# A fused attention and SwiGLU kernel: exponents of double-precision weights on ScalarE, and one batch's sum of squares on TensorE

## The chip, the cores and the metric

The kernel runs on one core of a Trainium2 chip. The metric is the device time of one execution in microseconds (us). The engines are TensorE (PE, with its weight loads as PEld), VectorE (DVE), ScalarE (ACT), GpSimd (POOL) and SyncE (SP), which issues most DMAs.

## The reference

Eight batches of 512 tokens and 32 state rows attend to each other over 8 heads of 64; the 544 rows of each batch then go through an RMS norm and a SwiGLU layer of width 1536. Inputs x and state are float32. The weights reach the kernel as 64-bit floating point, so each weight is two 32-bit words.

```python
scores = scale * x @ state.T;  a = softmax(scores);   xread = a @ state
scores2 = scale * state @ x.T; a2 = softmax(scores2); sread = a2 @ x
x = concat([xread, sread], axis=2)        # (8, 8, 544, 64) -> (4352, 512)
xn = x / sqrt(mean(x * x, -1) + 1e-6) * rms_g
g = xn @ w_gate; val = xn @ w_val         # (512, 1536) each
out = (g * sigmoid(g) * val) @ w_out      # (1536, 512)
```

## The kernel before

**Weights.** The three weight matrices are cut into 18 pieces of 128 partitions by 1024 values: 12 for the gate and value matrices, 6 for the output matrix. `load_piece` brings a piece in as pairs of 32-bit words (tile `raw`, four buffers; the word with index 1 holds sign, 11 exponent bits and 20 mantissa bits, the word with index 0 the low mantissa). `to_float32` makes float32 of it: VectorE shifts the exponent out (L183), ScalarE turns it into the inverted float32 exponent by two Relus (L185, L186), and ScalarE copies the low word as a scaled float32 (L188). VectorE then extracts the top mantissa bits and sets the hidden one (L189), adds the low part (L190), puts the sign into the exponent (L192) and multiplies mantissa by power of two (L196). `top` and `ex` have two buffers each. The first piece is done in two halves. Gate and value pieces go to `w_m` tiles in SBUF (three buffers) and, by a DMA, to a float32 copy in DRAM (`w_d`), from which later batches load them; output pieces stay in `wo`. `ready(n)` converts pieces up to number n, and is called by the code that needs them.

**Attention.** `attention(b)` is a generator whose steps are placed between the matmuls of the batch before. It transposes x (L232), makes scores (L240), softmaxes both ways, reads the states (L291, into four PSUM banks: two named `at`, two named `pv`), squares the reads on ScalarE (L297) and sums the squares. VectorE adds the four squares (L300, L301), and TensorE multiplies by a column of ones (L304) to sum over partitions. VectorE adds the epsilon (L307), GpSimd takes the power (L206), TensorE spreads it (L209), and VectorE scales the attention weights by it (L310). The other direction follows (L316 to L346).

**Feed-forward.** `make_v` multiplies the states by the weights (L381) into the `pv` banks, and ScalarE copies the result to `v` (L388). In batch 0, `hidden` multiplies `v` with the scaled attention weights (L407), applies tanh on ScalarE (L412) and gates on VectorE (L413, L415); `project_as_ready` multiplies with `wo` (L493). Later batches use a form with seven products (L445, L536). So all conversions, and the attention of batches 0 and 1, fall into batch 0's stage, up to about 140 us of the trace.

**Order.** Tiles and waits are placed by the framework, which also orders each engine's instructions when the program is built. The order in the trace is therefore not the order of the text: in the trace L316 at 31.87 us runs ahead of L300 at 35.53 us. Each engine then works in order.

Of the kernel before, what the change touches and what calls it, by code (L numbers as in the profile page):

```python
# [8 lines left out]
F32 = mybir.dt.float32  # L9
I32 = mybir.dt.int32  # L10
U32 = mybir.dt.uint32
ALU = mybir.AluOpType
ACTF = mybir.ActivationFunctionType
AXX = mybir.AxisListType.X
# [2 lines left out]
P = 128  # L17
# [5 lines left out]
def kernel(  # L23
# [20 lines left out]
    VE, SE, GE, TE = nc.vector, nc.scalar, nc.gpsimd, nc.tensor  # L44
# [15 lines left out]
    two = ctx.enter_context(tc.tile_pool(name="two", bufs=2))  # L60
# [35 lines left out]
    ones = consts.tile([P, 1], F32, name="ones")  # L96
    GE.memset(ones, 1.0)
    bounds = consts.tile([P, 2], F32, name="bounds")
    GE.memset(bounds[:, 0:1], 1151.0)
    GE.memset(bounds[:, 1:2], 255.0 * (1 << 23))  # L100
    rms_g = consts.tile([P, NI], F32, name="rms_g")

# [26 lines left out]
    def home(k):  # L129
        if k >= NM:  # L130
            m = 2 * (k - NM)
            return wo[:, m:m + 2].rearrange("p m (i f) -> p m i f", f=P)
        mp = k // 2
        return (w_sb[mp] if k % 2 else new_w(mp))[:, :, :, k % 2, :]

    def load_piece(k):
        if k >= len(pieces):
            return
        src = pieces[k]
        if src.dtype == F32:  # L140
            return
        raw[k] = raws.tile([P, 8 * P, 2], I32, name="raw")
        out_ = raw[k].rearrange("p (a f) two -> p a (f two)", a=src.shape[1])
        for a in parts(k):
            nc.sync.dma_start(out=out_[:, a], in_=src[:, a].bitcast(I32))

    def parts(k):

        n = pieces[k].shape[1]
        return (slice(0, n // 2), slice(n // 2, n)) if k == 0 else (slice(0, n),)  # L150
# [3 lines left out]
    def ready(n):  # L154

        nonlocal n_ready
        while n_ready < min(n, len(pieces)):
            k = n_ready
            to_float32(k)
            if k < NM and k % 2:  # L160
                nc.sync.dma_start(out=w_d[k // 2], in_=w_sb[k // 2])
            n_ready += 1

    def to_float32(k):


        load_piece(k + RAW_AHEAD)
        to = home(k)
        if k not in raw:
            src = pieces[k].rearrange("p a (c f) -> p a c f", f=P)  # L170
            for a in range(src.shape[1]):
                nc.sync.dma_start(out=to[:, a], in_=src[:, a])
            return
        whole = raw.pop(k)
        tops = conv.tile([P, 8 * P], I32, name="top")
        exs = conv.tile([P, 8 * P], I32, name="ex")
        n = pieces[k].shape[1]
        for a in parts(k):
            cols = slice(8 * P * a.start // n, 8 * P * a.stop // n)
            r, top, ex, dst = whole[:, cols, :], tops[:, cols], exs[:, cols], to[:, a]  # L180
            hi = r[:, :, 1]
            man = r.bitcast(F32)[:, :, 0]
            VE.tensor_scalar(ex, hi, 20, 0x7ff, op0=ALU.logical_shift_right, op1=ALU.bitwise_and)  # L183

            SE.activation(out=ex, in_=ex, func=ACTF.Relu, scale=-1.0, bias=bounds[:, 0:1])  # L185
            SE.activation(out=ex, in_=ex, func=ACTF.Relu, scale=-float(1 << 23),  # L186
                          bias=bounds[:, 1:2])
            SE.activation(out=man, in_=r.bitcast(U32)[:, :, 0], func=ACTF.Copy, scale=2.0 ** -52)  # L188
            VE.tensor_scalar(top, hi, 0xfffff, 0x100000, op0=ALU.bitwise_and, op1=ALU.bitwise_or)  # L189
            VE.scalar_tensor_tensor(out=man, in0=top, scalar=2.0 ** -20, in1=man,  # L190
                                    op0=ALU.mult, op1=ALU.add)
            VE.scalar_tensor_tensor(out=ex, in0=hi, scalar=-(1 << 31), in1=ex,  # L192
                                    op0=ALU.bitwise_and, op1=ALU.bitwise_or)
            man, ex = (t.rearrange("p (a c f) -> p a c f", f=P, c=dst.shape[2])
                       for t in (man, ex.bitcast(F32)))
            VE.tensor_tensor(out=dst, in0=man, in1=ex, op=ALU.mult)  # L196


    stT_g = {}
# [3 lines left out]
    def inverse_rms(ss, n):  # L203

        ri = two.tile([P, NC], F32, name="ri")
        GE.tensor_tensor(out=ri[:, 0:n], in0=ss, in1=mhalf[:, 0:n], op=ALU.pow)  # L206
        rp = aps.tile([P, NC, P], F32, name="at")
# [4 lines left out]
    def attention(b):  # L212
        xb, packed = x_sb.pop(b), rows.pop(b)
        if b + 1 < B:
# [7 lines left out]
                     in_=packed.rearrange("p e d -> p (e d)"), identity=ident)  # L222
        VE.tensor_copy(stT, tp)
        VE.tensor_tensor(out=stT_g[b], in0=stT, in1=rms_g.unsqueeze(2).to_broadcast([P, 4, Ns]),
                         op=ALU.mult)
# [11 lines left out]
        sp = [aps.tile([P, S], F32, name="at") for e in range(2)]  # L237
        for j in range(4):
            for e in range(2):
                TE.matmul(out=sp[e][Ns * j:Ns * j + Ns, :], lhsT=stT[D * e:D * e + D, j, :],  # L240
                          rhs=xT[j // 2][D * e:D * e + D, j % 2].rearrange("p c t -> p (c t)"),
                          start=True, stop=True)
# [12 lines left out]
        for cp in range(2):  # L255
            tp = aps.tile([P, 2, 2, P], F32, name="at")
            for c in range(2):
                for e in range(2):
# [6 lines left out]
                             op=ALU.subtract)  # L265
# [4 lines left out]
        for cp in range(2):  # L270
# [6 lines left out]
                             op=ALU.mult)  # L277
            tp = aps.tile([P, 2, 2, P], F32, name="at")
            for c in range(2):
                for e in range(2):  # L280
                    TE.transpose(out=tp[:, c, e, :],
                                 in_=eS[:, 2 * cp + c, e].rearrange("p j n -> p (j n)"),
# [6 lines left out]
        for j in range(4):  # L289
            for e in range(2):  # L290
                TE.matmul(out=reads[j][D * e:D * e + D, :],  # L291
                          lhsT=packed[Ns * j:Ns * j + Ns, e, :],
                          rhs=aT[Ns * j:Ns * j + Ns, e].rearrange("n c t -> n (c t)"),
                          start=True, stop=True)
        sq = [one.tile([P, 2, S], F32, name="sq%d" % i, tag=("xT1", "eS")[i]) for i in range(2)]
        for j in (2, 3, 0, 1):
            SE.activation(out=sq[j // 2][:, j % 2, :], in_=reads[j], func=ACTF.Square,  # L297
                          scale=DM ** -0.5)
        yield
        VE.tensor_tensor(out=sq[1], in0=sq[1], in1=sq[0], op=ALU.add)  # L300
        VE.tensor_tensor(out=sq[0][:, 0, :], in0=sq[1][:, 0, :], in1=sq[1][:, 1, :], op=ALU.add)  # L301
        sp = aps.tile([P, NC], F32, name="at")
        for c in range(NC):
            TE.matmul(out=sp[:, c:c + 1], lhsT=sq[0][:, 0, P * c:P * c + P], rhs=ones,  # L304
                      start=True, stop=True)
        ss = two.tile([P, NC], F32, name="ss")
        VE.tensor_scalar(ss, sp, 1e-6, None, op0=ALU.add)  # L307
        yield
# [2 lines left out]
                         in1=rp.unsqueeze(1).to_broadcast([P, 2, S]), op=ALU.mult)  # L311
# [7 lines left out]
        for e in range(2):  # L319
            SE.activation(out=e2[:, e], in_=sS[:, e], func=ACTF.Exp, scale=SCALE,  # L320
                          bias=s2[:, e:e + 1], accum_out=z2[:, e:e + 1])
# [11 lines left out]
        for e in range(2):  # L333
            for c in range(NC):
                for j in range(4):
                    h = 2 * j + e
                    TE.matmul(out=rp[Ns * j:Ns * j + Ns, e, :],
                              lhsT=e2T[:, e, c, Ns * j:Ns * j + Ns],
                              rhs=xb[:, c, D * h:D * h + D],
                              start=(c == 0), stop=(c == NC - 1))  # L340
        sr = two.tile([P, 2 * D], F32, name="sr")
        for e in range(2):
            VE.tensor_scalar(sr[:, D * e:D * e + D], rp[:, e, :], z2[:, e:e + 1], None,
                             op0=ALU.mult)
# [266 lines left out]
    for k in range(1, RAW_AHEAD):  # L611
        load_piece(k)
    steps = attention(0)
    while next(steps) != "tokens":
        pass
    make_v(0, 0)
    ready(4)
    states_read = steps
    steps = attention(1)
    for _ in states_read:  # L620
        pass
# [5 lines left out]
    for b in range(B):  # L627
        if b > 0:
            steps = attention(b + 1) if b + 1 < B else state_norm()
        else:  # L630
            for m in range(NM):
                if m % 2 == 0 and m + 2 < NM:
                    make_v(b, m // 2 + 1)
                v, _ = v_sb[b, m // 2]
                hidden(m, S, lambda e, k: v[:, e, m % 2, k, :],
                       [aT_s[b][:, e, :] for e in range(2)])
                some(3)

            def between(m):
                if m == NM - 4:  # L640
                    ready(len(pieces))
                    early.close()
                    open_late()
                    prepare(b + 1)

            project_as_ready(store_tokens(b), between)
            sums = weight_sums()
# [53 lines left out]
```

## Time and profile before

| what | value |
|---|---|
| median of 4 runs | 879.05 us (877.03 to 881.34) |
| the profiled execution | 880.2 us, span 878.4 us |
| mean granted TensorE clock | 0.966 |
| TensorE busy | 832.3 us, 95% of the span |
| VectorE busy | 473.5 us, 54% |
| ScalarE busy | 341.7 us, 39% |

The profile is one execution taken by the hardware profiler. A group line gives the line of the kernel, the engine, the operation, out<-in with shapes, and how often it ran; then the busy time, the mean length of one in ns, and the engine's idle time before it with what ended it. The granted clock is the share of TensorE's full speed. A float32 matmul appears as two passes, each with a weight load.

### The profile page before, as it was taken

What the parts mean: (1) busy time and instruction counts of PE and PEld (TensorE: products, weight loads), DVE (VectorE), ACT (ScalarE), POOL (GpSimd) and SP (SyncE); (2) the same over time, 40 slices, a digit from 0 to 9 for tenths busy, and PEclk for the clock granted to TensorE, in tenths of its full rate; (3) what the DMA queues carried; (4) which work ended last, traced back from release to release, by engine and by line L of the source; (5) the groups of instructions that cost most, each with busy time, mean ns of one, the idle gap of its engine ahead of it and who ended that gap; (6) DMA issues with size and microseconds to landing.
All of it is one profiled execution on the core that took longest, in us unless ns stands there. A gap on an engine that the chain in (4) does not pass through costs nothing.

```text
span 878.4 us, 12043 instructions
## 1 busy us (share of the span) xinstructions
PE 832.3 (95%) x4806; PEld 610.0 (69%) x4806; DVE 473.5 (54%) x749; ACT 341.7 (39%) x571; POOL 156.2 (18%) x215
## 2 busy tenths in 40 slices
PE   3597999999999999999999999999999999999997
PEld 2252544577877778777877787777877787788886
DVE  5899898269216841476226921694148623651231
ACT  5678472364125520563136412552056313520110
POOL 0000005131113211230123112221132022310000
PEclk9598899999999999999999999999999999999999
DMA  9777771231233203330243124220243012311310
GB/s 291 251 203 256 216 280 49 99 140 52 50 112 129 96 18 118 112 141 4 73 130 134 52 49 144 99 93 1 85 141 112 1 56 97 141 44 37 108 48 25
DMA packets 61592, 94.11 MB, mean 107 GB/s; under 512 B 38752, under 2 KB 46432, under 8 KB 54624
## 3 DMA queue, kind: packets, MB, share of 16 engines
q1 hardware_dynamic: 57376, 92.29, 31.6%
q10 hardware_dynamic: 4160, 1.05, 0.5%
q8 instruction: 38, 0.62, 0.3%
q14 instruction: 18, 0.15, 0.0%
HBM read 78.12 MB, written 15.20 MB: 106 GB/s over the span
## 4 chain that ended last, share of the span: by engine, by line
PE 79%; DVE 11%; ACT 6%; DMA 1%; issue 1%; SPq 0%; POOL 0%; ACTq 0%; DVEq 0%
PE f L536 30%; PE f L445 24%; PE f L407 8%; PE pv L381 5%; PE f L493 5%; PE at L232 2%; ACT sq L297 2%; PE at L240 1%; ACT e L320 1%; PE at L304 1%; DVE m L316 1%; PE at L327 1%; PE at L291 1%; DVE hb L475 1%; DVE hb L471 1%
## 5 line engine op out<-in xcount | busy, mean ns | idle before, releaser
L445 PE MATMUL f<-aT_s,v 128*128 128x256 f32 x504 | 131.9, 394 | 2.8 <-ACT g L462 2.8
L536 PE MATMUL f<-wo,hb 128*128 128x256 f32 x540 | 128.3, 396 | 0.0
L445 PEld LDWEIGHTS f<-aT_s,v 128*128 128x128 f32 x504 | 89.4, 189 | 52.9 <-issue 29.8
L536 PEld LDWEIGHTS f<-wo,hb 128*128 128x128 f32 x540 | 106.8, 200 | 17.7 <-ACT ot L556 1.9
L556 ACT COPY ot<-f 128x256 f32<-128x256 f32 x60 | 19.6, 375 | 195.6 <-PE f L536 186.5
L388 ACT COPY v<-pv 128x512 f32<-128x512 f32 x96 | 51.8, 591 | 113.0 <-PE pv L381 113.0
L536 PE MATMUL f<-wt,hs 128*128 128x256 f32 x360 | 89.0, 393 | 0.0
L396 POOL TENSOR_TENSOR vs<-v 128x256 f32<-128x256 f32 x42 | 30.5, 727 | 323.4 <-ACT v L388 323.4
L445 PE MATMUL f<-aT_t,vs 128*128 128x256 f32 x336 | 86.3, 379 | 0.0
L460 DVE TENSOR_TENSOR g<-g,f 128x512 f32<-128x512 f32 x42 | 28.8, 685 | 89.5 <-PE f L445 62.9
L536 PEld LDWEIGHTS f<-wt,hs 128*128 128x128 f32 x360 | 65.3, 191 | 16.5 <-issue 4.9
L561 DVE TENSOR_TENSOR ot<-ot,f 128x256 f32<-128x256 f32 x45 | 17.1, 418 | 104.5 <-issue 53.2
L381 PE MATMUL pv<-w_m,stT_g 64*32 64x512 f32 x768 | 66.9, 627 | 6.8 <-ACT sq L297 6.1
L445 PEld LDWEIGHTS f<-aT_t,vs 128*128 128x128 f32 x336 | 63.8, 190 | 9.5 <-issue 0.8
L470 ACT ACTIVATE hb<-g 128x1024 f32<-128x1024 f32 x42 | 44.4, 1058 | 34.5 <-DVE g L464 34.5
L471 DVE SCALAR_TENSOR_TENSOR hb<-hb,g 128x1024 f32<-128x1024 f32 x42 | 51.5, 1226 | 7.2 <-ACT hb L470 7.2
L407 PE MATMUL f<-aT_s,v 128*128 128x512 f32 x96 | 47.6, 635 | 2.3 <-ACT v L388 2.3
L206 POOL TENSOR_TENSOR ri<-ss,mhalf 128x4 f32<-128x4 f32 x8 | 9.4, 1179 | 190.8 <-DVE ss L307 150.0
L445 PE MATMUL f<-aT_t,v 128*128 128x256 f32 x168 | 43.1, 379 | 0.0
L445 PE MATMUL f<-aT_s,vs 128*128 128x256 f32 x168 | 43.1, 379 | 0.0
L493 PE MATMUL f<-wo,hb 128*128 128x512 f32 x96 | 41.6, 593 | 0.0
L407 PE MATMUL f<-xsT,w_m 128*128 128x256 f32 x192 | 41.6, 379 | 0.0
(114 smaller groups left out, 1255.7 us busy)
## 6 DMA issues: line engine op xcount, KB each, us to landing
w_m<-w_d SPq DMA_DIRECT2D x48, 1024.0 KB, 4.8
x_b<-in_x_dram SPq DMA_DIRECT2D x28, 256.0 KB, 4.1
out_dram<-ot SPq DMA_DIRECT2D x56, 128.0 KB, 1.8
raw<-in_moe_w_val_dram SPq DMA_DIRECT2D x6, 1024.0 KB, 6.5
w_d<-w_m SPq DMA_DIRECT2D x6, 1024.0 KB, 8.5
raw<-in_moe_w_out_dram SPq DMA_DIRECT2D x6, 1024.0 KB, 6.3
raw<-in_moe_w_gate_dram SPq DMA_DIRECT2D x5, 1024.0 KB, 6.9
x_b<-in_x_dram ACTq DMA_DIRECT2D x4, 256.0 KB, 4.8
```

What stands on the lines that cost most here:

```text
L232: TE.transpose(out=tp[:, c, :], in_=xb[:, c, P * j:P * j + P], identity=ident)
L381: TE.matmul(out=pv[e][Ns * j:Ns * j + Ns, :], lhsT=stT_g[b][D * e:D * e + D, j, :], rhs=w[D * e:D * e + D, j].rearrange("p m k f -> p (m k ...
L388: SE.copy(v[:, e].rearrange("p m k f -> p (m k f)"), pv[e])
L396: GE.tensor_tensor(out=vs[:, 0], in0=a21, in1=a22, op=ALU.add)
L407: TE.matmul(out=ps[:, 0:n], lhsT=lhs(i, k), rhs=r, start=(i == 0), stop=(i == len(rhs) - 1))
L445: TE.matmul(out=ps[:, i, :], lhsT=lhs[:, i, :], rhs=rhs, start=(start and i == 0), stop=True, skip_group_check=True)
L460: VE.tensor_tensor(out=g[:, :, 0, :], in0=g[:, :, 0, :], in1=ys, op=ALU.add)
L470: SE.activation(out=h, in_=gate, func=ACTF.Tanh, scale=0.5)
L471: VE.scalar_tensor_tensor(out=h, in0=h, scalar=1.0, in1=gate, op0=ALU.add, op1=ALU.mult)
L493: TE.matmul(out=op, lhsT=hb[:, m, P * r:P * r + P], rhs=wo[:, m, :], start=(m == 0), stop=(m == NM - 1))
L536: TE.matmul(out=ps[:, r, :], lhsT=lhs(k)[:, P * r:P * r + P], rhs=rhs(k), start=(start and r == 0 and k == 0), stop=(k == HM - 1), skip_gr ...
L556: SE.copy(kept[r], ps[:, r, :])
```

## The change

In `to_float32` VectorE's shift (L183) goes. ScalarE takes the absolute value of the high word read as a float32, then runs the first Relu on the upper 16 bits of the result, which hold the exponent and four mantissa bits, with a scale of one sixteenth and a bias that lets the conversion to an integer round those four bits off. ScalarE's copy of the low word (L188) goes as well: VectorE reads the low word as an unsigned integer in the step that adds it (L190), with the factor 2 to the power 32 instead of 2 to the power −20 on the top bits. The final product (L196) becomes an operation with a scalar factor of 2 to the power −52. Each piece then has three ScalarE and four VectorE instructions, where it had three and five.

In `attention`, batch 0 no longer adds its four squares on VectorE; TensorE multiplies each of the four with the column of ones and accumulates in PSUM, 16 matmuls instead of 4. Batches 1 to 7 are as before.

```diff
-    GE.memset(bounds[:, 0:1], 1151.0)
+    GE.memset(bounds[:, 0:1], 1151.0 + 7.5 / 16)
...
+            lo = r.bitcast(U32)[:, :, 0]
             man = r.bitcast(F32)[:, :, 0]
-            VE.tensor_scalar(ex, hi, 20, 0x7ff, op0=ALU.logical_shift_right, op1=ALU.bitwise_and)
-
-            SE.activation(out=ex, in_=ex, func=ACTF.Relu, scale=-1.0, bias=bounds[:, 0:1])
+            SE.activation(out=ex.bitcast(F32), in_=r.bitcast(F32)[:, :, 1], func=ACTF.Abs)
+            SE.activation(out=ex, in_=ex.bitcast(U16).rearrange("p (f two) -> p f two", two=2)[:, :, 1],
+                          func=ACTF.Relu, scale=-1.0 / 16, bias=bounds[:, 0:1])
             SE.activation(out=ex, in_=ex, func=ACTF.Relu, scale=-float(1 << 23),
                           bias=bounds[:, 1:2])
-            SE.activation(out=man, in_=r.bitcast(U32)[:, :, 0], func=ACTF.Copy, scale=2.0 ** -52)
             VE.tensor_scalar(top, hi, 0xfffff, 0x100000, op0=ALU.bitwise_and, op1=ALU.bitwise_or)
-            VE.scalar_tensor_tensor(out=man, in0=top, scalar=2.0 ** -20, in1=man,
+            VE.scalar_tensor_tensor(out=man, in0=top, scalar=2.0 ** 32, in1=lo,
                                     op0=ALU.mult, op1=ALU.add)
...
-            VE.tensor_tensor(out=dst, in0=man, in1=ex, op=ALU.mult)
+            VE.scalar_tensor_tensor(out=dst, in0=man, scalar=2.0 ** -52, in1=ex,
+                                    op0=ALU.mult, op1=ALU.mult)
...
-        VE.tensor_tensor(out=sq[1], in0=sq[1], in1=sq[0], op=ALU.add)
-        VE.tensor_tensor(out=sq[0][:, 0, :], in0=sq[1][:, 0, :], in1=sq[1][:, 1, :], op=ALU.add)
+        parts_ = [sq[j // 2][:, j % 2, :] for j in (2, 3, 0, 1)]
+        if b > 0:
+            VE.tensor_tensor(out=sq[1], in0=sq[1], in1=sq[0], op=ALU.add)
+            VE.tensor_tensor(out=parts_[2], in0=sq[1][:, 0, :], in1=sq[1][:, 1, :], op=ALU.add)
+            parts_ = [parts_[2]]
         sp = aps.tile([P, NC], F32, name="at")
         for c in range(NC):
-            TE.matmul(out=sp[:, c:c + 1], lhsT=sq[0][:, 0, P * c:P * c + P], rhs=ones,
-                      start=True, stop=True)
+            for i, part in enumerate(parts_):
+                TE.matmul(out=sp[:, c:c + 1], lhsT=part[:, P * c:P * c + P], rhs=ones,
+                          start=(i == 0), stop=(i == len(parts_) - 1))
```

More of the change, by code (lines that the diff above doesn't have):

```diff
@@ L11 @@
 U32 = mybir.dt.uint32
+U16 = mybir.dt.uint16
 ALU = mybir.AluOpType
```

## The prediction, made before the changed kernel was run

> **What bounds the kernel now.** I read the page first, its busy shares and its slices. Each digit is the busy tenth of a slice of 22 us.
>
> ```profile
> span 878.4 us, 12043 instructions
> ...
> PE 832.3 (95%) x4806; PEld 610.0 (69%) x4806; DVE 473.5 (54%) x749; ACT 341.7 (39%) x571; POOL 156.2 (18%) x215
> ...
> PE   3597999999999999999999999999999999999997
> ...
> DVE  5899898269216841476226921694148623651231
> ...
> PEclk9598899999999999999999999999999999999999
> ```
>
> TensorE is the bound of the whole and has no hole after the sixth slice. VectorE is full in the first six, where TensorE has holes and where the granted clock drops. The change touches only that part: the weights are converted there, and batch 0's attention lies there. So I asked for the busy time by stretches of 10 us, and quote four (PE, PEld, DVE, ACT and POOL busy, then the granted clock).
>
> ```profile
> 20.00:30.00 10.00, 2.17 (x8) 1.43 (x8) 10.00 (x17) 6.12 (x9) 0.00 (x0) 0.50 0.80 218
> 70.00:80.00 10.00, 7.18 (x36) 2.67 (x34) 10.00 (x21) 5.84 (x11) 0.00 (x0) 1.00 0.61 182
> 80.00:90.00 10.00, 7.09 (x28) 3.50 (x29) 8.01 (x11) 7.84 (x11) 0.80 (x1) 0.56 0.78 288
> 110.00:120.00 10.00, 8.39 (x38) 3.59 (x37) 9.92 (x13) 8.78 (x12) 0.00 (x0) 1.00 0.94 298
> ```
>
> VectorE is full wherever TensorE idles. Over 10 to 120 us TensorE idles 21.8 us (my sum of ten minus busy over the eleven stretches), and it runs at half clock from about 20 to 47 us and from 81.3 to 94.9 us. These holes and half-clock stretches are all that the change can win. The chain of waits says which VectorE work sets the end: from 57.7 to 78.1 us it lies on VectorE alone, and it holds the removed shift (L183) at 10.35 us (0.41), 18.18 (0.60), 59.46 (0.60), 61.20 (0.60) and 111.17 (0.61).
>
> Next come the groups of the first 130 us, each shape apart, for the prices: after the bar stand total busy us, the mean ns of one, and idle time before it.
>
> ```profile
> L188 ACT ACTIVATE raw<-raw 128x1024 f32<-128x1024 uint32 x17 | 19.4, 1165 | 0.0
> L190 DVE SCALAR_TENSOR_TENSOR raw<-top,raw 128x1024 f32<-128x1024 int32 x15 | 18.3, 1217 | 0.0
> L185 ACT ACTIVATE ex<-ex,bounds 128x1024 int32<-128x1024 int32 x15 | 17.2, 1146 | 6.5 <-DVE ex L183 6.5
> L196 DVE TENSOR_TENSOR w_m<-raw,ex 128x1024 f32<-128x1024 f32 x11 | 13.4, 1218 | 0.0
> L183 DVE TENSOR_SCALAR ex<-raw 128x1024 int32<-128x1024 int32 x15 | 10.3, 688 | 0.3 <-DMA raw<-in_moe_w_val_dram 0.3
> L304 PEld LDWEIGHTS at<-ones,sq 128*128 128x128 f32 x16 | 3.7, 330 | 2.7 <-DVE m L316 1.7 <-DVE sq L301 0.5 <-issue 0.5
> L304 PE MATMUL at<-ones,sq 128*128 128x1 f32 x16 | 3.6, 344 | 0.0
> ```
>
> **The change, part by part.** The sum is made against the profiled execution: 880.2 us, of which 878.4 is span. The median of the four runs is 879.05, or 1.15 lower. About 0.5% (4.4 us) is what a measurement of this kernel can tell from no change.
>
> *The shift leaves VectorE.* All of L183 is 12.6 us busy (17 of 688 ns, 2 of 428 ns); the next instruction starts 0.60 us after it, not 0.69. Only what lies on the chain counts: 0.41 + 0.60 + 0.60 + 0.60 = 2.2 us before 111 us. The upper bound is all of it before 120 us, 14 pieces at 0.60, or 8.4 us. I take 2.2, because in the other places the chain runs through TensorE or ScalarE and VectorE's shorter queue only ends earlier.
>
> *ScalarE waits for VectorE no more.* One place costs TensorE directly; here is its time line (start, length, engine, idle before).
>
> ```profile
> 111.08 0.69 DVE L183 TENSOR_SCALAR ex<-raw 128x1024 int32<-128x1024 int32 x1
> 111.81 1.15 ACT L185 ACTIVATE ex<-ex,bounds 128x1024 int32<-128x1024 int32 x1 [0.92 <-DVE ex L183]
> 112.87 1.05 ACT L388 COPY v<-pv 128x512 f32<-128x512 f32 x2
> 113.48 0.70 PE L407 MATMUL f<-aT_s,v 128*128 128x512 f32 x1 [1.60 <-ACT v L388]
> ```
>
> L185 waits for the shift, the copies of v stand behind it in ScalarE's queue, and TensorE stands 1.60 us. Their product (L381) was done at 111.3 us. Without the wait the copies come first, and TensorE reaches L407 when its transposes end at 111.9. I take 1.6 off; bounds 0 (an Abs of 1.17 us lands in the same place) and 1.6. What is late next is TensorE itself.
>
> *ScalarE's count stays.* Abs replaces Copy (L188): both read every second word of 1024 columns, so 1165 ns for 1165. The next Relu reads 16-bit halves: nearest row L185, 1146. VectorE's L190 with an integer in1 is nearest to L192 (1222), and the final product, now with a scalar, to L190 (1217 against 1218). All four at nothing; the bound either way is the spread of these rows, some 0.08 us a piece or 1.4 us in all, under VectorE's queue. The new order has one price: three ScalarE steps in series stand before the sign is put in (L192), 1.05 us for the Abs where the shift took 0.60. That is 0.45 a piece, hidden by the mantissa's steps on VectorE, which wait for ScalarE no longer; uncovered it is 18 times 0.45, or 8.1 us. L192 and the hidden-layer VectorE steps would queue behind it. Today L192 waits 0.8 us in all, so I take zero.
>
> *Batch 0's squares go to TensorE.* VectorE loses L300 (1.23) and L301 (0.69). TensorE gains 12 matmuls, each two passes in the trace (four columns are x8), so 24 passes and 24 weight loads. Prices: on the chain at half clock 8 passes took 1.79 us, 0.224 each; in a later batch at full clock 1.02, 0.128 each; if loads aren't hidden, 0.33 each from the row above. So 3.1, 5.4 or 7.9 us. I take 5.4, since the granted clock there is 0.50. Nothing of VectorE's 1.9 us returns, as TensorE did not stand for it: the sums were ready at 38.5 us, but L304 began at 40.13 behind L381. Two things return. TensorE's 0.72 us hole before 38.22 is filled. And TensorE is then unbroken from 35.06 instead of 38.22; full clock came 9 us after 38.22, so it may come 3.1 us earlier, which makes 3.1 us of work take half, 1.55. Net 5.4 − 0.7 − 1.6 = +3.1; ends 3.1 − 2.3 = +0.8 and +7.9. A net gain is excluded: those 2.3 us are all that the extra work can shorten.
>
> *The second clock drop.* TensorE's last matmul before it ended at 78.79; the next (L381) waited until 82.19 for the Squares (L297) to free its banks. The clock halved at 81.28, 2.5 us into the hole, and came back at 94.95. ScalarE did two Exps (L320, 1.43), two Squares, then a Relu (L185, 80.51, 1.04), and only then the Squares that count. If the hole is 0.9 us shorter, the clock stays. The Relu is 1.04 and ran there because its shift was issued at 78.60; the Abs needs only the loaded piece and a free buffer, which the product at 74.44 leaves at 75.6. So I expect it earlier, with its chain. Then the 12.0 us of TensorE's work between 81.28 and 94.95 (13.67 less holes of 0.91 and 0.72) takes 6.0, and the hole is 0.9 shorter: 6.9 us.
>
> The row for this clock is 2.5 us of idleness to drop and 9.6 us of work (from 85.35) to return. [...]
>
> Sum of the likeliest case: −2.2 − 1.6 + 3.1 − 6.9 = −7.6. From the profiled time 872.6, from the median **871.4 us**.
>
> **The rivals.**
>
> *The clock drop stays (no change).* If the Relu that moves away is replaced by an Abs, or L320 still sits ahead of the Squares, the 6.9 us are not won: −2.2 − 1.6 + 3.1 = −0.7, or 878.3. For it: only 0.1 us is to spare, and the order on ScalarE is made anew. ScalarE's longer chain taking back the 2.2 us belongs here too (+1.5). Against it: VectorE hands ScalarE work in bursts now, and ScalarE idles 2.8 us before 73.96.
>
> *The extra passes on TensorE decide (slower).* They lie between the Squares and batch 0's first hidden matmul (48.0 us), with TensorE unbroken until 72. If nothing of them is filled or shortened and the later stage stays as it is, only the first two shifts on the chain (1.0) return: at 0.224 a pass 5.4 − 1.0 = +4.4, at 0.33 a pass +6.9, so 883.4 to 885.9. It decides from 0.22 us a pass. For it: 330 ns is the measured mean of these loads, and the chain there runs through TensorE. Against it: TensorE stands 1.6 us in holes of the seventies, which absorb part.
>
> *Abs needs another table.* ScalarE loads a table once in the trace, 1.28 us. If every piece forced two loads, 36 times 1.28 is 46 us and the time 925. For it the trace has nothing, since it never runs Abs. [...]
>
> **How the numbers follow.** The likeliest case gets 0.48, no change 0.24, slower by the passes 0.26, the table 0.02. So faster by over 0.5% 0.48, within 0.24, slower 0.28. The likeliest case alone runs from 864 (the passes at +0.8, and 5 of the other 6.2 us of shifts won too) to 874 (the stall at 112 us kept, and 1.0 of the 1.4 us of spread against it). The range over all cases goes from 864 to 885: it leaves out the table, the upper tip of the slower case and what is better than 864, together under 2 in 10.
>
> **What would show it.** Right: L185 (now the Abs) never waits for VectorE; the granted clock is 1.00 throughout 80 to 95 us; no hole before L407 near 112 us; 32 passes of batch 0's sum take some 7 us at half clock. Wrong: a hole of 2.5 us or more between batch 1's reads and L381; L192 waiting for ScalarE by several us; more than one table load; TensorE's hole-free stretch beginning later than 120 us.

## The result and the profile after

The changed kernel takes 880.49 us, the median of 43 runs (877.77 to 883.93), against 878.10 for the kernel before (69 runs, 875.96 to 882.53). The ratio is 1.0023, interval 1.0016 to 1.0030. That is 0.23% slower, inside the 0.5% that the prediction cannot tell from no change, where 0.9% faster was forecast. The profiled executions alone would mislead: the changed kernel's took 878.2 us, near the lowest of its 43 runs, and that of before 880.2, above its median. So I compare stage by stage, and below a second profile of the changed kernel is added.

These lines of the changed kernel's page answer to those of before.

```profile
span 876.4 us, 12080 instructions
...
PE 835.4 (95%) x4830; PEld 611.5 (70%) x4830; DVE 462.3 (53%) x728; ACT 343.5 (39%) x571; POOL 151.3 (17%) x215
...
PE   3599999999999999999999999999999999999998
...
PEclk9569999999999999999999999999999999999999
```

VectorE is 11.2 us less busy, TensorE has 24 instructions more, and TensorE is full from the third slice on. But the third slice now shows a clock of 0.6, where it was 0.9 (slices are 22 us). The busy times by stretch (PE, PEld, DVE, ACT and POOL busy, then the granted clock) say the same:

```profile
20.00:30.00 10.00, 2.18 (x8) 1.44 (x8) 10.00 (x18) 7.67 (x10) 0.00 (x0) 0.54 0.67 174
50.00:60.00 10.00, 10.00 (x91) 3.78 (x90) 3.58 (x8) 5.62 (x9) 0.00 (x0) 0.58 0.17 38
80.00:90.00 10.00, 8.37 (x50) 3.42 (x51) 9.64 (x19) 9.08 (x16) 0.00 (x0) 1.00 0.52 218
110.00:120.00 10.00, 10.00 (x38) 4.16 (x23) 9.87 (x12) 9.55 (x12) 0.00 (x0) 1.00 0.97 327
```

TensorE is busy all through 50 to 60 us and still runs at half clock for most of it. Before, the same stretch ran at full clock:

```profile
50.00:60.00 10.00, 10.00 (x58) 5.06 (x66) 9.79 (x16) 7.42 (x11) 0.00 (x0) 1.00 0.79 211
```

The forecast effects are there too, in this trace: the clock holds at 80 to 90, and the hole at 112 us is closed. The groups of the first 130 us (total busy, mean ns, idle before) give the prices; the lines of the code moved, so L188 is now the Abs, L194 the added low word, L313 the sums on TensorE.

```profile
L188 ACT ACTIVATE ex<-raw 128x1024 f32<-128x1024 f32 x16 | 18.6, 1162 | 8.6 <-DVE w_m L200 5.4 <-DVE wo L200 3.2
L194 DVE SCALAR_TENSOR_TENSOR raw<-top,raw 128x1024 f32<-128x1024 int32 x15 | 18.4, 1224 | 0.0
L313 PEld LDWEIGHTS at<-ones,sq 128*128 128x128 f32 x40 | 7.9, 302 | 6.0 <-ACT sq L302 5.0 <-DVE sq L308 1.0
L188 ACT ACT_TABLE_LOAD x1 | 1.3, 1283 | 3.6 <-issue 3.6
```

The unit prices were right: 1162 ns for the Abs (1165 forecast), 1224 for the integer add (1222), one table load of 1283 ns, as in before. What went wrong is on TensorE. Its time line in the changed kernel (start, length, instructions, idle before) holds batch 0's sums and the first hidden matmul (L416, in before L407):

```profile
35.26 0.59 PE L313 MATMUL at<-ones,sq 128*128 128x1 f32 x2 [1.63 <-ACT sq L302]
35.77 1.93 PE L390 MATMUL pv<-w_m,stT_g 64*32 64x512 f32 x8
37.63 6.56 PE L313 MATMUL at<-ones,sq 128*128 128x1 f32 x30
44.12 1.91 PE L390 MATMUL pv<-w_m,stT_g 64*32 64x512 f32 x2
...
58.70 1.12 PE L416 MATMUL f<-aT_s,v 128*128 128x512 f32 x2
```

The same places in before:

```profile
35.06 2.44 PE L381 MATMUL pv<-w_m,stT_g 64*32 64x512 f32 x16 [2.66 <-ACT sq L297]
38.22 1.91 PE L381 MATMUL pv<-w_m,stT_g 64*32 64x512 f32 x2 [0.72 <-ACT v L388]
40.06 1.86 PE L304 MATMUL at<-ones,sq 128*128 128x1 f32 x8
41.85 1.91 PE L381 MATMUL pv<-w_m,stT_g 64*32 64x512 f32 x2
...
45.62 1.80 PE L381 MATMUL pv<-w_m,stT_g 64*32 64x512 f32 x12
...
47.85 1.02 PE L407 MATMUL f<-aT_s,v 128*128 128x512 f32 x2
```

In four milestones (us from the start of the span; "half clock" is the granted clock's record up to the project stage):

| kernel | first hidden matmul | reads of batch 0, batch 1 | first project matmul | half clock |
|---|---|---|---|---|
| before | 47.85 | 30.38, 77.68 | 120.45 | 19.8 to 47.1, 81.3 to 94.9 |
| after | 58.70 | 31.61, 86.28 | 120.36 | 20.8 to 58.3 |

The start of the hidden layer is 10.85 us late: 7.1 us of sums where 1.8 stood (+5.3); the products L390, broken into groups of 2, 6, 8 and 12, take 10.8 instead of 7.9 (+2.9); two groups of L346 that came later now lie ahead, at half clock (+2.0); the reads are 1.2 later, and 0.6 is won elsewhere. From there to batch 1's reads 2.25 us return, and from the reads to the first project matmul 8.7. The balance at 120 us is −0.1.

### The profile page after: what moved, and what is told of

Read it like the earlier page. It is cut to its first block, busy times and chain, and to the rows that moved or that the text cites. A ratio compares the mean times of both kernels' runs of the same rounds, so it can differ in the third digit from the quotient of the medians.

```text
span 876.4 us, 12080 instructions
## 1 busy us (share of the span) xinstructions
PE 835.4 (95%) x4830; PEld 611.5 (70%) x4830; DVE 462.3 (53%) x728; ACT 343.5 (39%) x571; POOL 151.3 (17%) x215
## 4 chain that ended last, share of the span: by engine, by line
PE 76%; DVE 12%; ACT 8%; issue 2%; DMA 1%; POOL 0%; SPq 0%; ACTq 0%; DVEq 0%; POOLq 0%
PE f L545 29%; PE f L454 23%; PE f L416 6%; PE pv L390 5%; PE f L502 5%; PE at L245 2%; PE at L237 2%; PE at L313 2%; ACT sq L302 1%; ACT e L329 1%; DVE hb L484 1%; DVE hb L480 1%; ACT hb L479 1%; DVE sq L307 1%; DVE m L325 1%
## 5 line engine op out<-in xcount | busy, mean ns | idle before, releaser
L545 PE MATMUL f<-wo,hb 128*128 128x256 f32 x540 | 126.2, 391 | 0.0
L570 DVE TENSOR_TENSOR ot<-ot,f 128x256 f32<-128x256 f32 x45 | 17.1, 418 | 104.5 <-issue 53.2
L390 PE MATMUL pv<-w_m,stT_g 64*32 64x512 f32 x768 | 70.2, 616 | 1.6 <-ACT sq L302 1.6
L416 PE MATMUL f<-aT_s,v 128*128 128x512 f32 x96 | 44.1, 600 | 0.0
L416 PE MATMUL f<-xsT,w_m 128*128 128x256 f32 x192 | 41.6, 379 | 0.0
```

The source lines that it names most:

```text
L390: TE.matmul(out=pv[e][Ns * j:Ns * j + Ns, :], lhsT=stT_g[b][D * e:D * e + D, j, :], rhs=w[D * e:D * e + D, j].rearrange("p m k f -> p (m k ...
L416: TE.matmul(out=ps[:, 0:n], lhsT=lhs(i, k), rhs=r, start=(i == 0), stop=(i == len(rhs) - 1))
L545: TE.matmul(out=ps[:, r, :], lhsT=lhs(k)[:, P * r:P * r + P], rhs=rhs(k), start=(start and r == 0 and k == 0), stop=(k == HM - 1), skip_gr ...
```

## The experiments

Theory: the conversion gains about what was forecast, and the sums lose as much again, because the half clock lasts longer. The rivals are that the conversion gains nothing by itself, and that the passes as such are the price, not the clock. Each ratio is against runs of the kernel before on the same chip.

**The change again, and the kernel before again,** each with its own profile.

> The changed kernel once more, for a second trace and for the same chip as the two halves. All theories: 0.2 to 0.3% slower than before. If the parts add, its difference from before is the sum of those of the two halves to within 1 us.

> The kernel before once more, for a second trace. Theory: the half-clock stretch from about 81 to 95 us shows again, the first hidden matmul starts within 1 us of 48 us, and where the time differs from the first trace, it differs by when the clock falls and returns. Rival: the second drop was a chance of the first trace and is not there, so that the changed kernel has won nothing by losing it.

The changed kernel: 880.77 us (12 runs), 1.0020 (1.0004 to 1.0036); its profiled execution 882.49. Hidden layer at 59.30, project at 122.91, half clock 20.7 to 61.7 and 92.4 to 95.8. Before, one run: 880.07, hidden layer 47.87, project 120.32, half clock 23.0 to 46.9 and 81.0 to 94.7. So before's stages repeat within some tenths. After's late hidden layer repeats too, but its undisturbed clock at 92 us does not: a stretch of 3.4 us came back. In this pair project starts 2.6 us late, about what the medians differ by. In the first pair it started at the same time, and the profiled change then came out ahead of before with three half-clock stretches of 3.4 us behind 120 us against five.

**Each part alone.** `conv_only` is the change with VectorE's two additions back in batch 0; `squares_only` is the kernel before with the sums of the change.

```diff
conv_only, against after
-        parts_ = [sq[j // 2][:, j % 2, :] for j in (2, 3, 0, 1)]
...
+        VE.tensor_tensor(out=sq[1], in0=sq[1], in1=sq[0], op=ALU.add)
+        VE.tensor_tensor(out=sq[0][:, 0, :], in0=sq[1][:, 0, :], in1=sq[1][:, 1, :], op=ALU.add)
```

> The conversion part of the change alone: exponents by Abs on ScalarE, low words as integers; batch 0's squares are added on VectorE as before. Theory (the squares on TensorE ate the gain): in the changed kernel's trace the first hidden matmul is 10.9 us late and all of that is given back by 120 us; without the squares the late start goes, so 868 to 873 us (0.989 to 0.994 of before), first hidden matmul near 48 us, no half clock after 50 us. Rival 1 (three ScalarE steps in series delay batch 0's attention): the late start stays with the conversion, 878 to 882 us. Rival 2 (order on the engines is made anew and the two parts don't add): 874 to 878 us.

> The other part alone: batch 0's four squares are summed on TensorE by 16 matmuls, the conversion is as before. Theory: 5.3 us for 24 more passes at half clock, plus up to 3 us for L381's groups of tiles being split by them: 882 to 888 us (1.005 to 1.011), with the second clock drop still there. Rival 1 (the late start comes from the conversion on ScalarE): within 1 us of before, 877 to 879. Rival 2: the longer unbroken work raises the clock earlier and pays, 876 to 878.

`conv_only`: 878.56 us, 1.0003 (0.9989 to 1.0018). `squares_only`: 885.75, 1.0077 (1.0052 to 1.0101). The sums cost 7.8 us of median; the conversion brings nothing, so that half of the theory is out. Together they cost 2.4, so they do not add. The time of `conv_only` is that of its rival 1, but the late start of that rival is not there: the hidden layer starts at 48.44 and project at 120.03; the hole at 112 us is closed, but the second half-clock stretch stays and is longer (81.0 to 98.1). Here are ScalarE and, in the last two lines, TensorE around batch 0's reads in `conv_only`:

```profile
28.01 1.16 ACT L188 ACTIVATE ex<-raw 128x1024 f32<-128x1024 f32 x1
29.21 1.15 ACT L189 ACTIVATE ex<-ex,bounds 128x1024 int32<-128x1024 uint16 x1
30.26 0.57 ACT L289 COPY aT_s<-at 128x512 f32<-128x512 f32 x1
```

```profile
30.88 1.13 PE L296 MATMUL at<-aT_s,rows 32*64 32x512 f32 x4 [1.80 <-ACT aT_s L289]
43.73 1.11 PE L214 MATMUL at<-ident,ri 128*128 128x128 f32 x4 [2.33 <-POOL ri L211]
```

Steps of the conversion that VectorE no longer holds back stand in ScalarE's queue ahead of the copy that the reads need; the hole before the reads is 1.80 us, 0.67 in before. And the clock, back at 40.1, drops at 43.5, in the 2.33 us hole, for 6.8 us. That is two windows of 3.4 us, the step in which it changes in all these traces: up to 120 us their half-clock stretches last from 3.4 to 41.0 us, each a multiple of it.

**The two halves of the conversion.** `exp_only` keeps the low words on ScalarE and changes only the exponent; `low_only` is the kernel before with only the low words moved.

```diff
exp_only, against conv_only
+            SE.activation(out=man, in_=lo, func=ACTF.Copy, scale=2.0 ** -52)
-            VE.scalar_tensor_tensor(out=man, in0=top, scalar=2.0 ** 32, in1=lo,
+            VE.scalar_tensor_tensor(out=man, in0=top, scalar=2.0 ** -20, in1=man,
low_only, against before
-            SE.activation(out=man, in_=r.bitcast(U32)[:, :, 0], func=ACTF.Copy, scale=2.0 ** -52)
-            VE.scalar_tensor_tensor(out=man, in0=top, scalar=2.0 ** -20, in1=man,
+            VE.scalar_tensor_tensor(out=man, in0=top, scalar=2.0 ** 32, in1=r.bitcast(U32)[:, :, 0],
```

(The final product takes or drops its factor of 2 to the power −52 with them.)

> Only the exponent path of the change (Abs, Relu on the 16-bit half, Relu); the low word is still copied by ScalarE, batch 0's squares are added by VectorE: four ScalarE and four VectorE instructions a piece. Theory (ScalarE's steps, now free to run, stand in front of batch 0's copies of the attention weights and eat what VectorE saves): the reads L296 (30.4 us before, 30.9 with the whole conversion part) start at 31 us or later, time 878 to 882. Rival (VectorE's shorter queue is worth its 3.8 us, the integer low words take it back): 873 to 876.

> Only the low words: VectorE adds them as integers, ScalarE's copy goes, VectorE's shift stays: two ScalarE and five VectorE instructions a piece; squares on VectorE. Theory: ScalarE has a third less to do, so the copies of the attention weights wait less and the reads start by 30 us; VectorE stays full, time 875 to 878, a little under before. Rival (integer operands make VectorE's step slower): L190 above 1.25 us, time 880 or more.

`exp_only`: 879.66, 1.0015 (1.0004 to 1.0027). `low_only`: 875.63, 0.9979 (0.9964 to 0.9994). Moving the exponents to ScalarE costs a little, taking the low words from it wins a little, and their sum is `conv_only`'s nothing. That would fit ScalarE as the engine to relieve, but it is not shown. In `exp_only` the hole before the reads is only 0.77 us, and TensorE waits 1.20 us at 39.29 for a converted piece instead. Where `low_only`'s 2 us lie is open: its project stage starts at 120.81, not before 120.45, and its profile has three half-clock windows behind 120 us where before's has five.

**The same sums with 128 columns.** `squares_wide` multiplies batch 0's squares with a 128x128 block of ones, so each matmul streams 128 columns instead of one; the other seven batches stay as in the change.

```diff
squares_wide, against squares_only
+        N = P if b == 0 else 1
-        sp = aps.tile([P, NC], F32, name="at")
+        sp = aps.tile([P, NC, N], F32, name="at")
-                TE.matmul(out=sp[:, c:c + 1], lhsT=part[:, P * c:P * c + P], rhs=ones,
+                TE.matmul(out=sp[:, c], lhsT=part[:, P * c:P * c + P],
+                          rhs=ones_w if b == 0 else ones,
```

> The squares-alone kernel with one change: batch 0's 16 summing matmuls stream 128 columns of ones instead of one column, with the same weight loads; the sum is read from the first column. Theory (passes of one column count as idleness for the clock): their time stays near 0.21 us a pass, but the clock comes back by 50 us instead of 56, and the time is 881 to 884 against 885.75. Rival (the clock follows unbroken occupancy, the passes cost by their number alone): clock back at 55 to 58 us, time 885 to 888.

Measured 877.73, 0.9995 (0.9984 to 1.0006): the whole 8 us are back. TensorE's time line, first of `squares_only`, then of `squares_wide`, and under each its stretch from 42 to 46 us (clock after the five engines):

```profile
38.09 6.56 PE L308 MATMUL at<-ones,sq 128*128 128x1 f32 x30
44.58 1.91 PE L385 MATMUL pv<-w_m,stT_g 64*32 64x512 f32 x2
...
55.87 1.23 PE L411 MATMUL f<-aT_s,v 128*128 128x512 f32 x2
```

```profile
42.00:46.00 4.00, 4.00 (x15) 2.73 (x14) 1.29 (x2) 0.00 (x0) 1.00 (x1) 0.50 0.00 0
```

```profile
38.52 5.99 PE L311 MATMUL at<-ones_w,sq 128*128 128x128 f32 x30
44.45 1.08 PE L389 MATMUL pv<-w_m,stT_g 64*32 64x512 f32 x14
...
50.49 1.13 PE L415 MATMUL f<-aT_s,v 128*128 128x512 f32 x2
```

```profile
42.00:46.00 4.00, 3.53 (x30) 2.50 (x29) 1.41 (x4) 0.39 (x1) 1.13 (x1) 0.81 0.96 355
```

The 32 passes take nearly as long (6.8 against 7.2 us), so their number is not by itself the price. With one column the clock stays at half for as long as they run, and on to 56.1; with 128 it returns at 43.5, during them. Up to there both kernels run the same matmuls in the same order, and a window that holds nothing but passes ends at half clock with one column (39.0 to 42.5 us) and at full clock with 128 (40.1 to 43.5). The products behind them then run 14 in 1.08 us instead of 2 in 1.91, and the hidden layer starts 5.4 us earlier.

**In between.** `squares_16` streams 16 columns (`N = 16`), to part width from order: with a wider tile the products also go through in one group behind the sums.

> The squares-alone kernel with 16 columns of ones instead of 128 in batch 0's summing matmuls; the passes cost their weight loads either way, and the order on TensorE is that of the 128-column kernel in all but two places. Theory (what counts for the clock is how many columns stream): clock back at 53 us or later, 883 to 886, like one column. Rival (the 128-column kernel gained by its other order of L381): 877 to 879, like 128 columns.

Measured 879.74, 1.0020 (1.0003 to 1.0037), between the two forecasts. The 32 passes take 7.2 us, as with one column, and the window from 39.4 to 42.8 us, which holds nothing else, leaves the clock at half. It returns at 49.6, behind the passes; 14 products go together at 45.46 in 1.95 us, and the hidden layer starts at 52.11. So 16 columns did not bring the clock back, and the 5 to 6 of the 8 us that come already with them point to the order behind the passes; the rest of the width brings 1 to 2. The order without any width was not run.

**No half clock in the softmax's hole.** `conv_warm` adds to `conv_only` eight matmuls of batch 0's scores with the identity, whose results are unused, just before TensorE's hole at 20 to 27 us.

```diff
+        if b == 0:
+            spare = [fx.tile([P, S], F32, name="f") for e in range(2)]
+            for i in range(8):
+                TE.matmul(out=spare[i % 2], lhsT=ident,
+                          rhs=sS[:, i % 2].rearrange("p c t -> p (c t)"), start=True, stop=True)
```

> The conversion part alone, with 8 matmuls of 512 columns into spare banks placed in TensorE's hole of batch 0's softmax (19 to 26 us); their result is not used. Theory (the half clock from 20 to 50 us is what the prologue loses): the clock stays at 1.00 through the hole or is back by 35 us, the first hidden matmul starts 3 to 6 us earlier than 48.4, time 873 to 876. Rival (TensorE's speed does not set the end there, VectorE's and ScalarE's chains do): 877.5 to 879.5, the first hidden matmul within 1 us of 48.4.

Measured 879.08, 1.0016 (1.0006 to 1.0025), as the rival had it. The clock now holds until 31.1, yet the reads come at 30.65 (30.88 in `conv_only`) and the hidden layer starts at 49.04. So the half clock in this hole is not what delays the reads; the clock falls right behind them, and again at 44.7.

**Width on the change itself.** `after_wide0` is the change with 128 columns in batch 0, `after_wide_all` in all batches; `before_wide_all` and `low_wide_all` are the kernel before and `low_only` with their four matmuls of sums 128 wide.

```diff
before_wide_all, against before
+    ones_w = consts.tile([P, P], F32, name="ones_w")
+    GE.memset(ones_w, 1.0)
-        sp = aps.tile([P, NC], F32, name="at")
+        sp = aps.tile([P, NC, P], F32, name="at")
-            TE.matmul(out=sp[:, c:c + 1], lhsT=sq[0][:, 0, P * c:P * c + P], rhs=ones,
+            TE.matmul(out=sp[:, c], lhsT=sq[0][:, 0, P * c:P * c + P], rhs=ones_w,
-        VE.tensor_scalar(ss, sp, 1e-6, None, op0=ALU.add)
+        VE.tensor_scalar(ss, sp[:, :, 0], 1e-6, None, op0=ALU.add)
```

> The changed kernel with one difference: batch 0's 16 summing matmuls stream 128 columns of ones instead of one. Theory (the one-column passes hold TensorE at half clock, and that is most of what the squares cost): clock back by 46 us instead of 58, first hidden matmul by 53 instead of 58.7, time 873 to 877 against 880.6. Rival (what the squares lost in the squares-alone kernel was its own order of instructions, and the changed kernel gives its late start back by 120 us anyway): 879 to 881.

> The same in all eight batches: 4 summing matmuls of 128 columns instead of one in batches 1 to 7. Theory: where the clock has dropped (batch 1, sometimes later ones) it comes back some us earlier, 0 to 3 us below the kernel with the wide sums in batch 0 alone; 871 to 876. Rival: wider passes cost their columns at full clock in seven batches, 1 to 2 us more.

> The kernel before, with 128 columns of ones in every batch's summing matmuls. Theory: its 8 one-column passes at 40 and 87 us sit in half-clock stretches too, and the clock comes back 2 to 5 us earlier in each: 874 to 877 against 878. Rival (4 matmuls are too few to matter): 877.5 to 878.5.

> The low words as integers alone, with 128 columns of ones in every batch's summing matmuls. Theory: the two gains add: 875.6 less 1 to 3, so 872 to 875. Rival (both act on the same half-clock stretch of batch 1): 875 to 876.

`after_wide0`: 878.10, 0.9994 (0.9981 to 1.0006). The clock is back at 40.5, the hidden layer starts at 49.08, 9.6 us earlier than in the change; of these only 2.4 us stay in the median; the second half-clock stretch is back (81.5 to 95.1). `after_wide_all`: 869.20, 0.9895 (0.9878 to 0.9913). `before_wide_all`: 870.23, 0.9912 (0.9894 to 0.9929). `low_wide_all`: 870.07, 0.9904 (0.9888 to 0.9921). These three came out below their forecasts. So wide sums alone, without anything of the change, take 0.9% off, and these beat both kernels. Most of that lies behind the prologue: `before_wide_all` reaches project 2.9 us earlier than before (117.52), but its span is 10.8 shorter (867.6). From 113 us of before on, the matmuls of both run in the same order but for four transposes. One place of a later batch shows how: before, then `before_wide_all`, each with the hole and the clock in the stretch that it leads into.

```profile
220.32 1.02 PE L304 MATMUL at<-ones,sq 128*128 128x1 f32 x8 [1.29 <-DVE sq L301]
```

```profile
222.00:226.00 4.00, 4.00 (x14) 3.23 (x14) 0.96 (x1) 0.65 (x2) 0.71 (x1) 0.67 0.00 0
```

```profile
217.83 1.13 PE L306 MATMUL at<-ones_w,sq 128*128 128x128 f32 x8 [1.29 <-DVE sq L303]
```

```profile
222.00:226.00 4.00, 4.00 (x28) 3.32 (x31) 1.22 (x1) 1.23 (x3) 0.45 (x1) 1.00 0.00 0
```

The hole is 1.29 us in both, but only the one followed by 1.02 us of one-column passes lets the clock fall for a window. In this pair the hole also lies at another place of its window, so one place proves little; the count is clearer. From 120 to 860 us the clock falls in none of the five kernels with all sums wide (two of them follow), and three to five times in each of the twelve other profiles. Over the whole span the mean granted clock is 0.966 in before and 0.982 in `before_wide_all`, or about 60 and 31 us at half clock (twice the missing share of the span). That is 29 us less, worth at most half of it.

**Each part again, all sums wide.**

> The conversion part alone, with 128 columns of ones in every batch's summing matmuls; to be set against the kernel before with wide sums (0.9912 of before). Theory (the conversion part moves work from VectorE to ScalarE's path in the prologue and wins little): 868 to 871, 0.989 to 0.992. Rival (its 3.8 us were there and hidden by the longer half-clock stretch at 82 us): 865 to 867.

> The squares part alone with 128 columns of ones in every batch. Theory (24 more passes, part at full clock, 3 to 5 us, less what the earlier clock returns): 870 to 874. Rival (with the clock kept the passes are hidden): 869 to 870.

`conv_wide_all` (`before_wide_all` with the conversion of the change): 873.90, 0.9945 (0.9927 to 0.9962). `squares_wide_all` (with the sums of the change): 871.59, 0.9913 (0.9892 to 0.9933). Beside 0.9912 for `before_wide_all` the conversion loses 0.33%, with intervals that just touch and a time above both forecasts, and the sums lose nothing. In `conv_wide_all` the clock returns at 42.3 and drops again at 45.7, in the same hole behind the sums as in `conv_only` (2.33 us in both, before the transposes of `ri`): that hole comes with the conversion, whatever the width. With both parts it is shorter (1.27 us in `after_wide0`), and the clock holds until 81 us.

## Why the prediction was wrong

**The step that failed** is "Batch 0's squares go to TensorE", and in it the clock's return. "0.224 each" for 24 passes gave 5.4, and the passes measured 0.22 us at half clock, so this size was right. But "full clock came 9 us after 38.22, so it may come 3.1 us earlier", −1.6, had the wrong sign. I took TensorE's unbroken run for what brings the clock back. In the change it is unbroken but for 0.43 us from 35.26 on, and the clock came at 58.3, 11.2 us later than before. A term was missing too: with the new passes the products L390 run in more and smaller groups, 10.8 us instead of 7.9, and the sum has nothing for that. Alone the part costs 7.8 us, where +3.1 was summed and +7.9 was its upper end. `squares_wide` gets all of it back, with the clock and the order that comes with it; `squares_16` gets most of it back while its clock stays at half through the passes. The second rival priced the part alone well (883.4 to 885.9; `squares_only` 885.75), but by the passes. Two kernels with as many passes take 877.73 and 879.74, so that agreement is luck. "Nothing of VectorE's 1.9 us returns" can't be judged: in the wide form the whole part costs nothing (0.9913 against 0.9912), with 24 more passes and without VectorE's additions.

**The clock's return.** I took "9.6 us of work", the trace's row, as a duration that carries over. It does not. All half-clock stretches up to 120 us, in the seventeen profiles, are whole windows of 3.41 us, among them 3.4 (1), 13.6 (4), 17.1 (5), 27.3 (8), 37.5 (11) and 41.0 us (12). In the traces of before and of the change so are the full-clock stretches between two drops, for example 34.1 (10), 126.3 (37) and 351.6 us (103). Nor did it suffice in the change that TensorE was busy. From 37.8 to 44.6 us two windows of almost nothing but one-column passes leave the clock at half. So do the three after them, to 54.9 us, with groups of 2 and 6 products, transposes, the small matmuls of L346 and a hole of 0.43 us. In `after_wide0` one window (37.1 to 40.5 us) with 2.8 us of 128-column passes brings it back. So in the change neither the one-column passes nor the work in those three windows brought the clock back. What exactly brings it back was not measured.

**The second drop (−6.9) and the hole at 112 us (−1.6).** From batch 1's reads to project the change won 8.7 us, 8.5 forecast. The size was right, the reason was not. I expected the Relu (L185) to move out from between the Squares. ScalarE in before, and then in the changed kernel:

```profile
78.13 0.72 ACT L320 ACTIVATE e<-sS,s 128x512 f32<-128x512 f32 x1 [0.50 <-DVE s L318]
...
78.85 0.71 ACT L320 ACTIVATE e<-sS,s 128x512 f32<-128x512 f32 x1
...
79.56 1.06 ACT L297 ACTIVATE sq<-at 128x512 f32<-128x512 f32 x2
80.51 1.14 ACT L185 ACTIVATE ex<-ex,bounds 128x1024 int32<-128x1024 int32 x1
81.55 1.07 ACT L297 ACTIVATE sq<-pv 128x512 f32<-128x512 f32 x2
```

```profile
79.31 0.71 ACT L329 ACTIVATE e<-sS,s 128x512 f32<-128x512 f32 x1
80.02 0.71 ACT L329 ACTIVATE e<-sS,s 128x512 f32<-128x512 f32 x1
...
87.40 1.09 ACT L302 ACTIVATE sq<-at 128x512 f32<-128x512 f32 x2 [0.38 <-PE pv L296]
88.37 1.09 ACT L302 ACTIVATE sq<-pv 128x512 f32<-128x512 f32 x2
```

The two Exps that stood between the reads and the Squares in before ran long ahead of the reads, because the reads came 8.6 us later; the hole fell from 3.40 to 1.63. That gain is the other side of the late hidden layer. Where the hidden layer is in time (`conv_only`, `after_wide0`), the hole (2.65 and 3.03) and the drop are back. There the Exps are out of the way, but an Abs stands where the Relu stood, in `conv_only`:

```profile
79.39 0.60 ACT L302 ACTIVATE sq<-at 128x512 f32<-128x512 f32 x1 [1.17 <-PE pv L296]
79.88 1.13 ACT L188 ACTIVATE ex<-raw 128x1024 f32<-128x1024 f32 x1
80.92 0.58 ACT L302 ACTIVATE sq<-at 128x512 f32<-128x512 f32 x1
```

That is the mechanism of the first rival ("the Relu that moves away is replaced by an Abs"). Its number, 878.3 beside 878.56 for `conv_only`, fits by luck: it holds +3.1 for sums that this kernel does not have. Nor does the row "2.5 us of idleness to drop" carry over. In `after_again` the clock fell at 92.4 behind a hole of 1.64 us, and in the change's first trace a hole of 1.63 us cost nothing.

**The shift (−2.2)** shows no gain of its own. From the hidden layer to batch 1's reads the change won 2.25 us, but `conv_only` has the same conversion and won nothing there (29.83 in both, though its first 1.9 us ran at half clock, worth 0.9 us). In it TensorE is unbroken from 48.4 to 77.6: VectorE gave up the chain and TensorE took it at once. For what is late next after this term I had named nothing. "VectorE is full wherever TensorE idles" was a misreading: from 30 to 40 and from 80 to 90 us it was busy 8.46 and 8.01 of 10 us, and TensorE waited there for ScalarE's Squares, 2.66 and 3.40 us.

**ScalarE's longer series, "I take zero",** was priced at the wrong place. It does not starve VectorE (L196 waits 2.2 us in all). But ScalarE's steps come earlier and stand before the copies for the reads, which cost 1.1 us of hole there in `conv_only` and in the change. What that hole is worth in the end was not measured alone. The sign "L185 (now the Abs) never waits for VectorE" did not come: the Abs waits 8.6 us for the products (L200) that free its buffers. **Table:** right, one load of 1.28 us.

## What to carry to other kernels

Ask of each TensorE stage not only if it is busy, but if it is busy with streamed columns. Here a window of nothing but one-column passes left the clock at half (`squares_only`, 39.0 to 42.5 us), and so did one of 16 columns (`squares_16`, 39.4 to 42.8); behind one of 128 columns it was back (`squares_wide`, at 43.5 us). Widening to columns that nobody reads cost nothing here: 32 passes took 6.8 us instead of 7.2, and `before_wide_all` 870.23 us where before takes 878.10. Two parts of a change that each move a queue's order should be forecast by their order, not by the sum of their prices. When a term takes work off a chain, name the engine that ties with it, or take zero.

## What the runs showed of the hardware

- At half clock a pass of a one-column fp32 matmul cost nearly what one of 128 columns cost here: 30 took 6.56 us in `squares_only`, and 5.99 in `squares_wide`, where about the last 1 us ran at full clock. Only in the second did the clock return during them, at 43.5 us.
- Small groups of tiled 64x512 products were dear at half clock here: 2 and 8 of them took 1.91 and 1.93 us in the change, 14 took 1.95 in `squares_16`.
- The phase of the clock's windows differed between executions: the first drops of the two profiles of before, at 19.84 and 22.99 us, lie 0.26 us short of a whole window apart, and those of `squares_only` and `squares_wide`, at 18.56 and 23.07 us, 1.10 us more than one. Both kernels scatter by some 6 us from lowest to highest; whether the phase is the cause was not shown.
- The clock's record can miss a stretch: in `exp_only` it shows full speed before 83.1 us, but four transposes (L332) took 1.06 us at 46.21 and 0.66 at 49.06; in before four of the same (L327) took 1.06 us at 44.63, at half clock, and 0.66 at 47.35, at full. Lengths of equal matmuls are the check.
